# Projecting keys and queries head by head, with high and low parts stacked on 128 partitions

## The chip, the cores and the metric

The kernel runs on one core of one Trainium2 chip. Its engines are TensorE (PE in the profile; PEld is its loading of weights, which overlaps the matmuls), VectorE (DVE), ScalarE (ACT), GpSimd (POOL) and SyncE (SP), which issues the DMAs here. The metric is device time in microseconds for one execution; lower is better.

## The reference

Linear attention for 8 batches of 8 heads, 576 positions, head dimension 64, 128 features, and then a feed-forward block with a gated depthwise convolution, all in float32:

```python
def phi(x):
    proj = np.einsum('bhsd,df->bhsf', x, w_phi)                  # 64 -> 128
    proj = proj - np.max(np.abs(proj), axis=-1, keepdims=True)
    return np.concatenate([np.exp(proj), np.exp(-proj)], axis=-1)
q_p, k_p = phi(q), phi(k)
kv = np.einsum('bhsf,bhsd->bhfd', k_p, v)
z = np.sum(k_p, axis=2)
num = np.einsum('bhsf,bhfd->bhsd', q_p, kv)
den = np.einsum('bhsf,bhf->bhs', q_p, z)[..., None] + 1e-06
x = num / den                                                    # heads joined: 576 x 512
h = np.maximum(x @ w_in, 0.0)                                    # 512 -> 1024
# conv_out: three taps of conv_w along the positions
out = (h / (1.0 + np.exp(-conv_out))) @ w_out                    # 1024 -> 512
```

The change concerns the first line of `phi`, for q and for k.

## The kernel before, in words

The host lays q and k out transposed, two heads above each other on the 128 partitions (64 dimensions each), and passes the projection weights as `wbd`, a 128 x 256 block-diagonal matrix: `w_phi` in the upper left for the first head, `w_phi` in the lower right for the second.

Most products are made in float32r, a data type that TensorE multiplies in one pass with fewer bits. To keep the accuracy each operand is split into a high part (rounded to float32r) and a low part (what is left), and three products are added up in PSUM: high by high, high by low, low by high. Some products use plain float32 instead; the profile then shows two records for each matmul. The profile prints `f32` for both types when it comes to TensorE.

The work of a batch is cut into two units `qd`, and each unit into five chunks `g`: chunk 0 has one block of 128 columns, chunks 1 to 4 have two blocks each, so a unit has nine blocks for k and nine for q. A block holds 128 positions of two heads. For each chunk:

- `load_split` (L180, L183) loads the chunk on SP's queue, and POOL makes the high part (L62, `kxh`, `qxh`) and the low part (L65, `kxl`, `qxl`). For q in the first two units (`NQ_F32`) there is no split.
- `project` multiplies. The data are the stationary operand (the weights of the PE array), `wbd` is the moving one. A block takes three matmuls of 256 columns (L203, L204, L205), or one in plain float32 (L200). DVE then takes the greatest absolute value (L208) and subtracts it (L210).
- For k, ACT takes the two exponentials, and TensorE multiplies with v into `kv` (L255, L259, plain float32).
- For q, TensorE transposes (L324), ACT takes the exponentials, high and low parts are made, and TensorE forms numerator and denominator `nm` (L352 plain float32, L360 float32r). The `kv` matmuls of the unit after are put between these by hand, by an order chain (`after`).

The denominators go by DMA into one small tile (L381), DVE takes reciprocals, and a DMA brings them back (L402); TensorE spreads them over the partitions (L410). Then the feed-forward block follows for half a batch at a time: 96 matmuls `hp` (L435), ReLU on ACT (L442) into a ring of `NH` tiles, the convolution on POOL and DVE (L458, L463), the sigmoid, the gating, and 96 matmuls `op` (L494). Its weights arrive as 64-bit words; POOL, DVE and ACT convert and split them during the first part of the run (`weight_process`, tile `w_t`).

The order in which all this is issued comes from a planner in the kernel file: generators for each chunk announce how long TensorE will be busy (`yield pe(330 * n)` for a projection of n blocks) and what they wait for, and the planner takes attention and feed-forward steps in proportion to what is left of each (`ATT_PE`, `MOE_PE`). The framework's scheduler then orders each engine's queue by these priorities.

Of the kernel before, what the change touches and what calls it, by code (L numbers as in the profile page):

```python
# [16 lines left out]
F = 128  # L17
# [6 lines left out]
NH = 11  # L24
# [11 lines left out]
def kernel(  # L36
# [44 lines left out]
    selr_f = sb.tile([P, P], F32, name="selr_f", tag="qr", bufs=2)  # L81
# [75 lines left out]
    def pe(ns):  # L157
        return ("pe", ns)
# [17 lines left out]
    def load_split(src, b, qd, g, kind):  # L176
        c0, n = group_columns(g)
        if kind == "q" and 2 * b + qd < NQ_F32:
            raw = sb.tile([P, n * P], F32, name=f"{kind}r{b}_{qd}_{g}", tag=kind + "xh", bufs=2)
            nc.sync.dma_start(out=raw, in_=src[b, qd, :, c0 : c0 + n * P])  # L180
            return n, raw, None
        raw = sb.tile([P, n * P], F32, name=f"{kind}r{b}_{qd}_{g}", tag=kind + "r", bufs=2)
        nc.sync.dma_start(out=raw, in_=src[b, qd, :, c0 : c0 + n * P])  # L183
# [5 lines left out]
    def project(n, hi, lo, b, qd, g, kind):  # L189

        if b == 0 and kind == "k":

            ps = pm.tile([P, n * 256], F32, name=f"{kind}p{b}_{qd}_{g}", tag="m")
        else:
            ps = pg.tile([P, n * 256], F32, name=f"{kind}p{b}_{qd}_{g}", tag="g", bufs=4)
        for t in range(n):
            o = ps[:, t * 256 : (t + 1) * 256]
            his = hi[:, t * P : (t + 1) * P]
            if lo is None:
                nc.tensor.matmul(out=o, lhsT=his, rhs=wbd_f, start=True, stop=True)  # L200
                continue
            los = lo[:, t * P : (t + 1) * P]
# [10 lines left out]
    def after(ins, trace):  # L213
# [3 lines left out]
        with tc.issue_after(ins.ins):  # L217
            return trace()
# [430 lines left out]
```

## Time and profile before

| | |
|---|---|
| time, median of 3 runs | 837.99 us (837.19 to 838.23) |
| the profiled execution, span from its first to its last instruction | 955.3 us (no other time of that execution is given) |
| mean granted TensorE clock in the profile | 0.750 of full speed |
| busy: PE, PEld, DVE, ACT, POOL | 937.9, 920.7, 622.2, 576.6, 294.1 us |
| instructions | 18005, of them 6414 matmuls and 6414 weight loads |

The profiled execution is longer than the timed runs; the profile says at which clock it ran, and nothing says so for the timed runs. Matmuls are pipelined: the duration of a matmul's record overlaps its neighbours', so the mean duration of a group isn't what a matmul costs. The cost is read from runs of matmuls one after another, from the chain of work that ended last, or from a window's share. In rows of groups the columns are line, engine, operation, tiles, shapes (for TensorE: weight rows x weight columns, then rows x moving columns), count, busy us, mean ns, idle time before and who ended it.

### The profile page before, as it was taken

The numbers are of one execution on the slowest core, as the hardware profiler recorded it, in microseconds if no ns is written. First come the engines' busy times: TensorE is split into PE (matmuls) and PEld (weight loads), VectorE is DVE, ScalarE is ACT, GpSimd is POOL, SyncE is SP. The second block draws the span as 40 slices with busy tenths as digits, with TensorE's granted clock in tenths as the row PEclk, the third lists the DMA queues.
The fourth block names the chain that finished last, engine by engine and source line by source line (L and its number), as shares of the span: only waits on it lengthen the run. The fifth ranks groups of instructions, "written<-read, shape, count | busy, mean of one in ns | idle before, by whom it ended". The sixth has DMA issues, their size and how long they took to land.

```text
span 955.3 us, 18005 instructions
## 1 busy us (share of the span) xinstructions
PE 937.9 (98%) x6414; PEld 920.7 (96%) x6414; DVE 622.2 (65%) x1326; ACT 576.6 (60%) x1228; POOL 294.1 (31%) x469
## 2 busy tenths in 40 slices
PE   8999899999999999999999999999999999999998
PEld 7887799999999999999999999999999999999998
DVE  6789986887767557576665656756667575555441
ACT  4787876866667555765647556675666647533322
POOL 5668753433323213131322312313123220111010
PEclk8677777777777777777777777777777777777777
DMA  5543321112112111111211101121111100000001
GB/s 169 173 136 117 96 57 47 41 37 58 40 49 58 33 50 38 44 54 31 57 32 52 53 25 56 37 62 38 39 52 28 38 5 21 15 19 26 20 20 37
DMA packets 56336, 49.19 MB, mean 51 GB/s; under 512 B 15028, under 2 KB 54200, under 8 KB 56248
## 3 DMA queue, kind: packets, MB, share of 16 engines
q1 hardware_dynamic: 56248, 48.05, 17.5%
q8 instruction: 51, 0.84, 0.4%
q14 instruction: 37, 0.30, 0.1%
HBM read 38.14 MB, written 9.44 MB: 50 GB/s over the span
## 4 chain that ended last, share of the span: by engine, by line
PE 93%; DVE 3%; ACT 2%; issue 1%; DMA 1%; POOL 0%; SPq 0%; ACTq 0%
PE op L494 26%; PE hp L435 25%; PE kv L259 10%; PE nm L360 9%; PE tp L324 4%; PE nm L352 3%; PE kp L203 2%; PE kp L204 2%; PE kp L205 2%; PE qp L204 2%; PE qp L203 2%; PE qp L205 2%; PE kv L255 2%; PE rb L410 1%; PE qp L200 1%
## 5 line engine op out<-in xcount | busy, mean ns | idle before, releaser
L259 PEld LDWEIGHTS kv<-v,ke 128*128 128x128 f32 x1024 | 181.8, 221 | 5.2
L259 PE MATMUL kv<-v,ke 128*128 128x65 f32 x1024 | 181.8, 280 | 0.0
L463 DVE SCALAR_TENSOR_TENSOR c<-h,cw,c 128x287 f32<-128x287 f32 (+1 forms) x256 | 138.6, 550 | 59.1 <-POOL c L458 57.3
L435 PE MATMUL hp<-xl,win_hi 128*128 128x290 f32 x512 | 171.0, 334 | 0.0
L435 PE MATMUL hp<-xh,win_hi 128*128 128x290 f32 x512 | 170.9, 335 | 0.1
L494 PE MATMUL op<-gh,wout_hi 128*128 128x288 f32 x512 | 170.5, 333 | 0.0
L494 PE MATMUL op<-gh,wout_lo 128*128 128x288 f32 x512 | 170.3, 333 | 0.0
L494 PE MATMUL op<-gl,wout_hi 128*128 128x288 f32 x512 | 170.3, 333 | 0.0
L435 PE MATMUL hp<-xh,win_lo 128*128 128x290 f32 x512 | 170.1, 332 | 0.0
L458 POOL TENSOR_SCALAR c<-h,cw 128x288 f32<-128x288 f32 x128 | 73.0, 571 | 264.1 <-ACT h L442 234.6
L62 POOL TENSOR_SCALAR kxh<-kr 128x256 fp32r<-128x256 f32 (+1 forms) x80 | 38.6, 482 | 259.0 <-PE kp L204 252.6
L65 DVE TENSOR_TENSOR ql<-qe,qh 128x512 fp32r<-128x512 f32 x112 | 77.6, 707 | 45.7 <-ACT qh L60 45.6
L435 PEld LDWEIGHTS hp<-xh,win_hi 128*128 128x128 f32 x512 | 104.4, 205 | 1.0 <-ACT os L499 0.6
L435 PEld LDWEIGHTS hp<-xh,win_lo 128*128 128x128 f32 x512 | 104.2, 204 | 0.2
L435 PEld LDWEIGHTS hp<-xl,win_hi 128*128 128x128 f32 x512 | 103.6, 202 | 0.2
L494 PEld LDWEIGHTS op<-gh,wout_hi 128*128 128x128 f32 x512 | 103.7, 203 | 0.0
L494 PEld LDWEIGHTS op<-gh,wout_lo 128*128 128x128 f32 x512 | 103.5, 202 | 0.1
L442 ACT ACTIVATE h<-hp 128x290 f32<-128x290 f32 x128 | 52.4, 411 | 84.4 <-PE hp L435 83.9
L494 PEld LDWEIGHTS op<-gl,wout_hi 128*128 128x128 f32 x512 | 103.2, 202 | 0.1
L378 ACT ACTIVATE dr<-nm 1x512 f32<-1x512 f32 (+1 forms) x96 | 46.3, 483 | 77.7 <-PE nm L360 48.6
L208 DVE TENSOR_REDUCE km<-kp 128x4 f32<-128x512 f32 (+1 forms) x80 | 50.6, 633 | 59.5 <-PE kp L205 59.1
L330 ACT ACTIVATE qe<-tp 128x512 f32<-128x512 f32 x112 | 61.7, 597 | 39.0 <-PE tp L324 37.3
(88 smaller groups left out, 2125.1 us busy)
## 6 DMA issues: line engine op xcount, KB each, us to landing
v<-in_vt_dram SPq DMA_DIRECT2D x80, 130.0 KB
out_dram<-os SPq DMA_DIRECT2D x64, 144.0 KB
qr<-in_qT_dram SPq DMA_DIRECT2D x64, 128.0 KB
kr<-in_kT_dram SPq DMA_DIRECT2D x64, 128.0 KB
w_r<-in_w_in_dram SPq DMA_DIRECT2D x8, 512.0 KB
w_r<-in_w_out_dram SPq DMA_DIRECT2D x8, 512.0 KB
rr<-rc SPq DMA_DIRECT2D x128, 2.2 KB
qr<-in_qT_dram SPq DMA_DIRECT2D x16, 64.0 KB
```

What stands on the lines that cost most here:

```text
L62: nc.gpsimd.tensor_scalar(out=hi, in0=src, scalar1=1.0, scalar2=0.0, op0=ALU.mult, op1=ALU.add)
L65: eng_lo.tensor_tensor(out=lo, in0=src, in1=hi.bitcast(F32), op=ALU.subtract)
L208: nc.vector.tensor_reduce(out=m, in_=ps3, axis=AX, op=ALU.max, apply_absolute_value=True)
L259: ins = nc.tensor.matmul(out=kp[i][:, s, p0 : p0 + VW], lhsT=lhsT, rhs=v[:, (2 * t + i) * VW : (2 * t + i + 1) * VW], start=False, stop=(g ...
L330: nc.scalar.activation(out=e, in_=tp.rearrange("p i t s -> p i (t s)"), func=AF.Exp, scale=1.0 - 2.0 * s)
L360: ins = after(ins, lambda: nc.tensor.matmul(out=ps[:, i, o : o + w], lhsT=w_, rhs=x_, start=(k == 0), stop=(k == 5)))
L378: nc.scalar.activation(out=dro.rearrange("o (r i c) -> o i r c", i=2, c=16), in_=ps[D : D + 1, :, o : o + w].rearrange("o i (r c) -> o i r ...
L435: nc.tensor.matmul(out=ps, lhsT=w_, rhs=x_, start=(k == 0), stop=(k == 11))
L442: nc.scalar.activation(out=hs, in_=ps, func=AF.Relu)
L458: nc.gpsimd.tensor_scalar(out=cv, in0=hs[:, o : o + TC], scalar1=cw[:, f, 1:2], scalar2=0.0, op0=ALU.mult, op1=ALU.add)
L463: nc.vector.scalar_tensor_tensor(out=cv[:, lo:hi], in0=hs[:, o + j - 1 + lo : o + j - 1 + hi], scalar=cw[:, f, j : j + 1], in1=cv[:, lo:hi ...
L494: nc.tensor.matmul(out=ps, lhsT=w_, rhs=x_, start=(k == 0), stop=(k == 23))
```

## The change

Each head is projected by itself. A block's data are laid out so that one head's high part stands on partitions 0 to 63 and its low part on partitions 64 to 127, 128 columns. Stacked so, one pass against `w_phi`'s high part written twice above itself gives high by high plus low by high, and a second pass against the low part written twice gives high by low plus low by low. A block of two heads takes four matmuls of 128 moving columns, where three of 256 stood.

For that, each chunk is loaded twice, once to the upper and once to the lower 64 partitions, with the two heads side by side in the columns (two DMAs, each of the full size). POOL makes the high part over all 128 partitions and twice the columns, and then the low part over the lower 64 partitions and twice the columns. The weights come by three DMAs into one tile, `wst_f`, and are split into `wst`, high part left, low part right. In the plain float32 chunks the same doubled layout is multiplied with `w_phi` above zeros. The raw tiles of k and q share one ring of three (`r`), where each kind had two. The ring of `h` tiles goes from 11 to 10. The planner's figure for a projection goes from 330 to 225 a block. `after` is only moved in the file.

```diff
-NH = 11
+NH = 10
...
-    wbd_f = cp.tile([P, 2 * F], F32, name="wbd_f")
+    wst_f = cp.tile([P, 2 * F], F32, name="wst_f")
     with tc.high_priority():
-        nc.sync.dma_start(out=wbd_f, in_=wbd)
-    wbd_hi = cp.tile([P, 2 * F], F32R, name="wbd_hi")
-    wbd_lo = cp.tile([P, 2 * F], F32R, name="wbd_lo")
-    split(wbd_f, wbd_hi, wbd_lo, nc.vector, nc.vector)
+        nc.sync.dma_start(out=wst_f[:D, :F], in_=wbd[:D, :F])
+        nc.sync.dma_start(out=wst_f[D:, :F], in_=wbd[D:, F:])
+        nc.sync.dma_start(out=wst_f[:, F:], in_=wbd[:, :F])
+    wst = cp.tile([P, 2 * F], F32R, name="wst")
+    split(wst_f[:, :F], wst[:, :F], wst[:, F:], nc.vector, nc.vector)
...
     def load_split(src, b, qd, g, kind):
         c0, n = group_columns(g)
+        w = 2 * n * P
+
+        def load(raw):
+            for h in range(2):
+                nc.sync.dma_start(out=raw[D * h : D * h + D].rearrange("d (i c) -> d i c", i=2),
+                                  in_=src[b, qd, :, c0 : c0 + n * P].rearrange("(i d) c -> d i c", i=2))
+
         if kind == "q" and 2 * b + qd < NQ_F32:
-            raw = sb.tile([P, n * P], F32, name=f"{kind}r{b}_{qd}_{g}", tag=kind + "xh", bufs=2)
-            nc.sync.dma_start(out=raw, in_=src[b, qd, :, c0 : c0 + n * P])
-            return n, raw, None
-        raw = sb.tile([P, n * P], F32, name=f"{kind}r{b}_{qd}_{g}", tag=kind + "r", bufs=2)
-        nc.sync.dma_start(out=raw, in_=src[b, qd, :, c0 : c0 + n * P])
-        hi = sb.tile([P, n * P], F32R, name=f"{kind}xh{b}_{qd}_{g}", tag=kind + "xh", bufs=2)
-        lo = sb.tile([P, n * P], F32R, name=f"{kind}xl{b}_{qd}_{g}", tag=kind + "xl", bufs=2)
-        split(raw, hi, lo, nc.gpsimd, nc.gpsimd)
-        return n, hi, lo
+            raw = sb.tile([P, w], F32, name=f"{kind}r{b}_{qd}_{g}", tag=kind + "x", bufs=2)
+            load(raw)
+            return n, raw
+        raw = sb.tile([P, w], F32, name=f"{kind}r{b}_{qd}_{g}", tag="r", bufs=3)
+        load(raw)
+        x = sb.tile([P, w], F32R, name=f"{kind}x{b}_{qd}_{g}", tag=kind + "x", bufs=2)
+        nc.gpsimd.tensor_scalar(out=x, in0=raw, scalar1=1.0, scalar2=0.0, op0=ALU.mult, op1=ALU.add)
+        nc.gpsimd.tensor_tensor(out=x[D:], in0=raw[D:], in1=x[D:].bitcast(F32), op=ALU.subtract)
+        return n, x
...
-        for t in range(n):
-            o = ps[:, t * 256 : (t + 1) * 256]
-            his = hi[:, t * P : (t + 1) * P]
-            if lo is None:
-                nc.tensor.matmul(out=o, lhsT=his, rhs=wbd_f, start=True, stop=True)
-                continue
-            los = lo[:, t * P : (t + 1) * P]
-            nc.tensor.matmul(out=o, lhsT=his, rhs=wbd_hi, start=True, stop=False)
-            nc.tensor.matmul(out=o, lhsT=his, rhs=wbd_lo, start=False, stop=False)
-            nc.tensor.matmul(out=o, lhsT=los, rhs=wbd_hi, start=False, stop=True)
+        for j in range(2 * n):
+            t, i = divmod(j, 2)
+            o, xs = ps[:, j * F : (j + 1) * F], x[:, (i * n + t) * P : (i * n + t + 1) * P]
+            if x.dtype == F32:
+                nc.tensor.matmul(out=o, lhsT=xs, rhs=wst_f[:, F:], start=True, stop=True)
+            else:
+                nc.tensor.matmul(out=o, lhsT=xs, rhs=wst[:, :F], start=True, stop=False)
+                nc.tensor.matmul(out=o, lhsT=xs, rhs=wst[:, F:], start=False, stop=True)
...
-        yield pe(330 * n)
+        yield pe(225 * n)
...
-    ATT_PE = B * (18 * 330 + 72 * 215 + 18 * 550 + 8 * 6 * 270 + 4 * 250)
+    ATT_PE = B * (18 * 225 + 72 * 215 + 18 * 550 + 8 * 6 * 270 + 4 * 250)
```

More of the change, by code (lines that the diff above doesn't have):

```diff
@@ L71, in load_const @@
         return t
-    wbd_f = cp.tile([P, 2 * F], F32, name="wbd_f")
+    wst_f = cp.tile([P, 2 * F], F32, name="wst_f")
     with tc.high_priority():
-        nc.sync.dma_start(out=wbd_f, in_=wbd)
-    wbd_hi = cp.tile([P, 2 * F], F32R, name="wbd_hi")
-    wbd_lo = cp.tile([P, 2 * F], F32R, name="wbd_lo")
-    split(wbd_f, wbd_hi, wbd_lo, nc.vector, nc.vector)
+        nc.sync.dma_start(out=wst_f[:D, :F], in_=wbd[:D, :F])
[3 more added lines that the diff above has]
+    split(wst_f[:, :F], wst[:, :F], wst[:, F:], nc.vector, nc.vector)
     idn = load_const(ident, [P, P], "idn")
-    selr_f = sb.tile([P, P], F32, name="selr_f", tag="qr", bufs=2)
+    selr_f = sb.tile([P, P], F32, name="selr_f", tag="r", bufs=3)
     nc.gpsimd.memset(selr_f, 0.0)
@@ L177, in load_split, with after, project @@
         c0, n = group_columns(g)
-        if kind == "q" and 2 * b + qd < NQ_F32:
-            raw = sb.tile([P, n * P], F32, name=f"{kind}r{b}_{qd}_{g}", tag=kind + "xh", bufs=2)
-            nc.sync.dma_start(out=raw, in_=src[b, qd, :, c0 : c0 + n * P])
-            return n, raw, None
-        raw = sb.tile([P, n * P], F32, name=f"{kind}r{b}_{qd}_{g}", tag=kind + "r", bufs=2)
-        nc.sync.dma_start(out=raw, in_=src[b, qd, :, c0 : c0 + n * P])
-        hi = sb.tile([P, n * P], F32R, name=f"{kind}xh{b}_{qd}_{g}", tag=kind + "xh", bufs=2)
-        lo = sb.tile([P, n * P], F32R, name=f"{kind}xl{b}_{qd}_{g}", tag=kind + "xl", bufs=2)
-        split(raw, hi, lo, nc.gpsimd, nc.gpsimd)
-        return n, hi, lo
-    def project(n, hi, lo, b, qd, g, kind):
+        w = 2 * n * P
[3 more added lines that the diff above has]
+                                  in_=src[b, qd, :, c0 : c0 + n * P].rearrange("(i d) c -> d i c", i=2))
+        if kind == "q" and 2 * b + qd < NQ_F32:
+            raw = sb.tile([P, w], F32, name=f"{kind}r{b}_{qd}_{g}", tag=kind + "x", bufs=2)
[7 more added lines that the diff above has]
+        return n, x
+    def after(ins, trace):
+        if ins is None:
+            return trace()
+        with tc.issue_after(ins.ins):
+            return trace()
+    def project(n, x, b, qd, g, kind):
         if b == 0 and kind == "k":
@@ L211, in project @@
         return pr
-    def after(ins, trace):
-        if ins is None:
-            return trace()
-        with tc.issue_after(ins.ins):
-            return trace()
     kv = {}
@@ L230, in k_process @@
         yield until(back("kp", 2), back("kv", 4))
-        n, hi, lo = load_split(kT, b, qd, g, "k")
+        n, x = load_split(kT, b, qd, g, "k")
         v0 = 16 if g == 0 else 4 * (g - 1)
@@ L237, in k_process @@
         set_ready(("kp", j))
-        pr = project(n, hi, lo, b, qd, g, "k")
+        pr = project(n, x, b, qd, g, "k")
         e = sb.tile([P, 2, 2 * n, F], F32, name=f"ke{b}_{qd}_{g}", tag="ke", bufs=2)
@@ L310, in q_process @@
         yield until(back("qp", 2))
-        n, hi, lo = load_split(qT, b, qd, g, "q")
+        n, x = load_split(qT, b, qd, g, "q")
         yield wait(3000)
@@ L314, in q_process @@
         set_ready(("qp", *divmod(j, 5)))
-        pr = project(n, hi, lo, b, qd, g, "q")
-        yield pe(330 * n)
+        pr = project(n, x, b, qd, g, "q")
+        yield pe(225 * n)
         yield wait(1700)
```

## The prediction

> **What bounds the kernel now.** I read the page first: span, the busy share of each engine, the chain that ended last.
>
> ```profile
> span 955.3 us, 18005 instructions
> PE 937.9 (98%) x6414; PEld 920.7 (96%) x6414; DVE 622.2 (65%) x1326; ACT 576.6 (60%) x1228; POOL 294.1 (31%) x469
> PE 93%; DVE 3%; ACT 2%; issue 1%; DMA 1%; POOL 0%; SPq 0%; ACTq 0%
> ```
>
> TensorE is nearly always busy and carries 93% of the chain. The weight loads (PEld) are busy almost as long as the matmuls, and there is one load for each matmul: 6414 and 6414. So I ask which of the two ends last where the projections run. Next the busy times by stretch (columns: window, its length, PE, PEld, DVE, ACT, POOL busy with counts, granted clock, DMA share, GB/s), then the chain of 200 to 830 us and the counts of projection matmuls in it.
>
> ```profile
> 48.00:100.00 52.00, 49.43 (x295) 42.35 (x294) 45.24 (x82) 41.64 (x88) 39.01 (x41) 0.74 0.43 124
> ...
> 200.00:830.00 630.00, 630.00 (x4451) 628.04 (x4450) 407.32 (x894) 391.65 (x838) 163.90 (x293) 0.75 0.15 41
> ```
>
> ```profile
> by line: PE op L494 27.0%; PE hp L435 26.9%; PE nm L360 12.1%; PE kv L259 11.1%; PE tp L324 4.5%; PE qp L204 2.4%; PE qp L203 2.3%; PE kp L204 2.2%; PE qp L205 2.2%; PE kp L203 2.1%; PE nm L352 2.0%; PE kp L205 2.0%; PE kv L255 1.9%; PE rb
> L203 PE MATMUL qp<-wbd_hi,qxh 128*128 128x256 f32 x99 | 31.3, 326 | 0.0
> L203 PE MATMUL kp<-wbd_hi,kxh 128*128 128x256 f32 x92 | 31.1, 339 | 0.0
> ```
>
> From 200 to 830 us TensorE has no gap at all at a granted clock of 0.75, while DVE, ACT and POOL are busy for 407, 392 and 164 of 630 us. There a nanosecond of TensorE is a nanosecond of the kernel. The six projection lines take 2.4+2.3+2.2+2.2+2.1+2.0 = 13.2% of that stretch, 83.2 us, for 191 blocks (99+92) of three matmuls: 435 ns a block, 145 ns a matmul. The mean durations of the matmul rows (326 and 339 ns) overlap and are not this cost.
>
> **What a matmul costs on this chip.** The windows' columns here are PE busy, PEld busy, clock; the next two rows are from the chain (start, length, what), the last three the weight loads (shortest/median/longest ns).
>
> ```profile
> 19.94:21.96 2.02, 2.02 (x14) 1.98 (x14) 0.75 0.07 12
> 28.07:31.27 3.20, 3.20 (x16) 3.20 (x16) 0.50 0.47 166
> ```
>
> ```profile
> 140.35 0.58 PE nm L352 x8
> ```
>
> ```profile
> 441.85 9.44 PE op L494 x59
> ```
>
> ```profile
> L259 PEld LDWEIGHTS kv<-v,ke x1024: 186/225/338, 13.4 to 773.3; 128*128 128x128 f32 x171
> L360 PEld LDWEIGHTS nm<-qh,kvh x224: 134/139/227, 101.8 to 819.5; 128*65 128x65 f32 x112
> L203 PEld LDWEIGHTS kp<-wbd_hi,kxh x144: 186/198/338, 5.1 to 762.1; 128*128 128x128 f32 x144
> ```
>
> Streaming: the op run is 9.44 us for 59 matmuls of 288 columns, 160 ns each, 0.556 ns a column; so 256 columns stream in 142 ns and 128 in 71 ns. Loading: the first two rows are back-to-back kv matmuls (L259), 65 moving columns against 128 weight columns: 2.02/14 = 144 ns each at clock 0.75 and 3.20/16 = 200 ns at 0.50. The nm run (L352) has the same data type and 64 moving columns, but 65 weight columns: 0.58/8 = 72 ns. Nearly the same stream, half the weights, half the time: the kv run goes at the pace of its weight loads, 144 ns for 128 weight columns. Does a float32r load cost the same as the plain float32 of kv? The projections' load (L203) is 186 ns at the shortest, kv's 186, and the 65-column float32r load (L360) 134. The two 128-column kinds agree, so I take 144 ns for both. A matmul's slot is then the longer of its own stream and of the load of the next one's weights. The present projection sits at balance: stream 142, next load 144, measured 145.
>
> The Trainium skill, "TensorE: Matmul & The Clock Gate", section "LDWEIGHTS (loading the stationary operand)", gives a load as columns / 1.2 ns, 107 ns for 128 columns; divided by the clock of 0.75 this is an estimate of 142 ns, and the kv row agrees.
>
> **The change, part by part.**
>
> *Projection matmuls.* A block (128 columns of two heads) goes from three matmuls of 256 columns to four of 128: 768 streamed columns to 512, but three weight loads to four. The two matmuls on the same x slice don't share a load: L203 and L204 share hi now, and the loads number as many as the matmuls. A new slot is 144 ns where the next weights are 128 wide, 72 ns where they are the 65 of nm. How often that is, the chain shows:
>
> ```profile
> 405.02 0.15 PE kp L203
> 405.18 0.15 PE kp L204
> 405.33 0.17 PE kv L259 x2
> 405.50 0.18 PE kp L205
> 405.68 0.12 PE nm L360
> 405.80 0.15 PE kp L203
> 405.95 0.17 PE kv L259 x2
> 406.12 0.22 PE qp L203
> 406.33 0.16 PE qp L204
> 406.49 0.12 PE qp L205
> 406.61 0.16 PE qp L203
> 406.77 0.15 PE kp L204
> 406.92 0.12 PE nm L360
> ```
>
> Of nine projection matmuls two are followed by nm. With that mix a block costs 4 x (7/9 x 144 + 2/9 x 72) = 512 ns against 435: +77 ns. There are 144 + 126 = 270 float32r blocks (16 units of nine, less two units of q in plain float32): +20.8 us. Upper end: every successor is 128 wide, 576 ns, +141, +38 us. Lower end: every second successor short, 432 ns, -3 ns, -1 us. I take the 77, the rate of the row.
>
> *The plain float32 q blocks* (two units, L200):
>
> ```profile
> L200 PE MATMUL qp<-wbd_f,qr 128*128 128x256 f32 x36 | 12.8, 496 | 4.6 <-DMA qr<-in_qT_dram 4.1 <-ACT qh L330 0.5
> ```
>
> 36 records for 18 blocks: two a matmul, at nm's 72 ns per 64 columns 288 ns each, 576 a block. After: two heads x two records of 128 columns, 144 ns of stream, 144 of load: 576. Nothing.
>
> *Splits on POOL and loads.* hi is made over twice the columns, lo over twice the columns on half the partitions.
>
> ```profile
> L62 POOL TENSOR_SCALAR kxh<-kr 128x256 fp32r<-128x256 f32 x64 | 32.6, 509 | 221.6 <-PE kp L204 218.6 <-DMA kr<-in_kT_dram 2.1 <-PE kv L255 0.8
> L62 POOL TENSOR_SCALAR kxh<-kr 128x128 fp32r<-128x128 f32 x16 | 6.0, 376 | 37.4 <-PE kp L204 34.0 <-DMA kr<-in_kT_dram 3.2
> L65 POOL TENSOR_TENSOR kxl<-kr,kxh 128x256 fp32r<-128x256 f32 x64 | 51.0, 797 | 3.4 <-PE kp L205 1.0
> L109 POOL TENSOR_TENSOR w_t<-w_t 128x512 f32<-128x512 f32 x16 | 22.7, 1417 | 11.1 <-DVE w_t L107 7.4 <-DMA rr<-rc 3.0 <-DVE rc L64 0.6
> 48.00:100.00 52.00, 9.59 (x14) 0.74 0.43 124
> 48.00:100.00 52.00, 5.27 (x16) 3.04 (x16) 6.60 (x11) 0.74 0.43 124
> ```
>
> Hi at 512 columns: 509 + 2 x (509 - 376) = 775 ns; lo: the 512-column subtraction row, 1417. A chunk goes from 1306 to 2192 ns, +0.9 us; the 120 large chunks make 106 us, the 30 small ones less than a fifth of that. From 200 us on POOL has 466 idle us and its splits wait for TensorE (218.6 us): hidden. From 48 to 100 us it is not so clear: POOL is busy 39.0 of 52, and the last two rows (what touches kr; what touches qr) show 14 + 11 split instructions, 12.5 chunks, +11.3 us: 50.3 of 52, beside the weight conversion on the same queue. I take +3 us, ends 0 (the 13 idle us take it) and +8 (most of the 11.3 shows, since DVE, at 45 of 52, waits on POOL's results too).
>
> ```profile
> L183 SPq DMA_DIRECT2D kr<-in_kT_dram x80: 327/339/1165, 2.1 to 719.8; - x80
> ACT h L442 <- PE hp L435: 83.9, 68, 2.7
> ```
>
> Each chunk's load becomes two DMAs of full size: 160 more issues at 0.34 us, 54 us on SP's queue, at a DMA share of 0.15 in the long stretch: hidden. The raw tiles go from two per kind to three for both; SP waits for POOL to free one, and with POOL slower it will wait longer, with the stores and the den and rr transfers queued behind. DVE waits for den, TensorE after it; the zero gaps of TensorE cover that, and I cost it at nothing, +5 us if that cover goes. At the start, two more small weight loads and one more issue ahead of the first q and k chunk: 3 x 0.34, +1 us. NH 11 to 10: the h copies on ACT wait for TensorE alone (second row), not for a buffer; nothing, and at worst a short wait of ACT under TensorE's other work. The planner's 225 for 330 only reorders TensorE's queue, which is full in either order. The split of the weights halves two DVE instructions at the start: nothing.
>
> **Sum.** In the profiled execution +20.8 + 3 + 1 = 24.8 us on a span of 955.3; no own time stands beside the span. The median of the runs is 837.99, 0.877 of it; no row shows their clock. Since TensorE's time goes with the clock, I scale its term: 20.8 x 0.877 = 18.2, and leave the other 4: 838 + 22 = 860 us. Its own range: PE -1 to +33, the rest 0 to +10, 837 to 881.
>
> **The rivals.**
>
> *Columns decide, faster.* If the narrow float32r matmuls' loads hide better than kv's, a block costs 4 x 71 = 284 ns, -151, -40.8 us, scaled -35.8: with the 4 us above, 806. For it: the total stream falls and no row shows a float32r load binding by itself. Against: the 186 ns floor shared by both kinds. It decides once a load falls below 435/4 = 109 ns.
>
> By the Trainium skill, same page, section "Back-to-back issue gap", a warm matmul takes N/2.4 + 2.5 ns, 55.8 for 128 columns and 109.2 for 256; as an estimate 4 x 55.8 against 3 x 109.2, so this rival. The kv row, 144 ns for 65 columns, does not follow that formula.
>
> *Interleaving covers the loads, about no change.* The scheduler mixes projections with nm and kv; at every second successor short a block is level (432 ns), and only POOL and the start remain: 838 to 846.
>
> *Narrow float32r runs like plain float32, much slower.* Every float32r matmul in this trace streams at least 256 columns. If 128 columns run as the L200 rows do, in two records, a block has eight slots of 144: 1152, +717, +194 us, scaled +170: about 1012. For it speaks only that no row excludes it.
>
> **How the numbers follow.** Forecast 0.60; columns decide 0.16; covered 0.15 (0.04 faster, 0.05 same, 0.06 slower); like float32 0.09. About 0.2% (1.7 us) is what a measurement of this kernel tells from no change. Faster 0.16 + 0.04 = 0.20, same 0.05, slower 0.60 + 0.06 + 0.09 = 0.75. The range reaches down to 822, where about half of the first rival's chance lies above it, and up to 884: left out are 0.09 and about 0.08.
>
> **What would show it.** Projection loads x1080 with a 186 ns floor, and projection lines that take more of the chain in the long stretch (above 15%) with 125 to 145 ns a matmul: the load bound. Near 75 ns a matmul: the first rival. Two records a matmul: the last. POOL near 50 of 52 us between 48 and 100 with TensorE's gaps grown there: the POOL term. I am wrong if float32r loads of this shape run faster than kv's, or if the order pairs them with nm far more often.

## The result, and the profile after

The changed kernel takes 890.80 us (median of 4 runs, 887.75 to 893.78) against 837.59 us (4 runs, 836.79 to 838.23) on the same chip: a ratio of 1.0637 (95% interval 1.0612 to 1.0663), 53 us slower. The forecast was 860 us, with a range of 822 to 884: the sign is right, the time lies above the range.

The profile of before that the prediction read ran at a clock of 0.75. To compare at one clock, the unchanged kernel was profiled again (`e0_before`, below: 838.14 us, span 836.4, clock 0.986). The changed kernel's profiled run took 890.75 us, span 888.9, clock 0.964. First the page of the changed kernel, then that of the unchanged one: span, busy times, the chain that ended last.

```profile
span 888.9 us, 18763 instructions
PE 836.7 (94%) x6720; PEld 823.3 (93%) x6720; DVE 676.8 (76%) x1326; ACT 570.8 (64%) x1228; POOL 421.9 (47%) x469
PE 61%; DVE 18%; ACT 8%; DMA 6%; issue 4%; POOL 2%; SPq 1%; POOLq 0%; ACTq 0%; DVEq 0%
```

```profile
span 836.4 us, 18005 instructions
PE 799.5 (96%) x6414; PEld 781.4 (93%) x6414; DVE 623.8 (75%) x1326; ACT 573.0 (69%) x1228; POOL 308.1 (37%) x469
PE 77%; DVE 8%; ACT 7%; DMA 4%; issue 3%; POOL 1%; SPq 0%; POOLq 0%; DVEq 0%; ACTq 0%
```

TensorE is busy for 37.2 us more and idle for 15.3 us more (52.2 against 36.9). In the traces of these two runs the granted clock is always either 0.5 or 1.0, so the means of 0.964 and 0.986 are 64 and 23 us at half clock; of the 37.2 us up to 20 are that (an estimate, as if TensorE had work in all of it). The timed runs agree: 0.960 to 0.967 in the changed kernel, 0.979 to 0.990 in the unchanged one. The 306 further matmuls are the 270 of the float32r blocks and 36 records of the plain float32 q blocks. DVE runs the same 1326 instructions, yet is busy for 53 us more, and its share of the chain goes from 8% to 18%. That was in no step of the prediction. The stretches (window in us, its length, PE, PEld, DVE, ACT, POOL busy, clock, DMA share, GB/s) show where; the changed kernel first, then the unchanged one.

```profile
0.00:30.00 30.00, 18.60 (x121) 18.35 (x122) 9.09 (x18) 7.40 (x15) 14.66 (x24) 0.94 0.52 146
30.00:120.00 90.00, 72.64 (x506) 66.05 (x506) 75.66 (x128) 64.82 (x139) 65.84 (x59) 0.86 0.53 159
120.00:200.00 80.00, 74.20 (x585) 72.44 (x585) 75.32 (x132) 56.72 (x121) 59.27 (x56) 0.88 0.33 93
200.00:300.00 100.00, 95.79 (x797) 94.61 (x796) 82.85 (x165) 72.10 (x157) 48.78 (x56) 0.97 0.26 72
300.00:700.00 400.00, 392.61 (x3307) 391.00 (x3306) 315.03 (x629) 272.27 (x586) 196.29 (x221) 0.99 0.25 72
```

```profile
0.00:30.00 30.00, 21.56 (x136) 19.36 (x137) 19.86 (x39) 14.13 (x28) 16.59 (x33) 0.94 0.61 181
30.00:120.00 90.00, 73.97 (x504) 63.66 (x503) 78.34 (x137) 72.76 (x153) 65.78 (x65) 0.91 0.42 123
120.00:200.00 80.00, 75.58 (x632) 73.99 (x630) 70.92 (x148) 62.63 (x137) 37.72 (x57) 0.98 0.19 51
200.00:300.00 100.00, 98.45 (x839) 97.86 (x838) 79.00 (x170) 73.13 (x160) 37.79 (x61) 1.00 0.20 57
300.00:700.00 400.00, 397.61 (x3316) 395.36 (x3315) 300.29 (x660) 286.27 (x615) 133.48 (x223) 1.00 0.17 48
```

Up to 300 us TensorE has made 2009 matmuls in the changed kernel and 2111 in the unchanged one, although the changed one needs more of them for the same work. In this early part DVE was close to full already (70.9 of 80 us between 120 and 200 us) and is now at 75.3, and the granted clock falls (0.86 and 0.88 against 0.91 and 0.98). Two neighbouring pieces of the changed kernel show what that does:

```profile
125.70:139.30 13.60, 10.50 (x93) 9.83 (x92) 13.60 (x20) 11.42 (x23) 13.18 (x10) 1.00 0.37 101
139.30:153.00 13.70, 11.99 (x62) 11.54 (x60) 13.51 (x22) 7.03 (x16) 11.56 (x11) 0.50 0.41 124
```

DVE is busy throughout, TensorE has gaps in the first piece, and in the second, at half clock, it makes 62 matmuls where it made 93. Here a lost wait seems to be paid twice, once as a gap and once as slower matmuls behind it; no run isolates this. The Trainium skill, "TensorE: Matmul & The Clock Gate", section "HAM oscillation — how this bites in real kernels", ties a halved clock to gaps of TensorE longer than about 3.4 us. The halving agrees, the length of the gap does not: between 126 and 153 us no wait of TensorE was over 2.0 us.

The matmul count is also a ledger (a running account of who is behind) for those experiments that keep the number of matmuls: the unchanged kernel makes 3316 in 400 us, 0.121 us each, and what another kernel is behind at 300 us and again at 700 us, times 0.121, is its loss by stage.

### The profile page after: what moved, and what is told of

Read it like the earlier page. It is cut to its first block, busy times and chain, and to the rows that moved or that the text cites. A ratio compares the mean times of both kernels' runs of the same rounds, so it can differ in the third digit from the quotient of the medians.

```text
span 888.9 us, 18763 instructions
## 1 busy us (share of the span) xinstructions
PE 836.7 (94%) x6720; PEld 823.3 (93%) x6720; DVE 676.8 (76%) x1326; ACT 570.8 (64%) x1228; POOL 421.9 (47%) x469
## 4 chain that ended last, share of the span: by engine, by line
PE 61%; DVE 18%; ACT 8%; DMA 6%; issue 4%; POOL 2%; SPq 1%; POOLq 0%; ACTq 0%; DVEq 0%
PE op L504 19%; PE hp L445 18%; PE nm L370 6%; PE kv L269 6%; PE tp L334 3%; DMA den<-dr 2%; PE kp L221 2%; PE kp L222 2%; PE qp L222 2%; PE qp L221 2%; DVE qm L225 2%; DVE ql L65 2%; DVE km L225 2%; DVE c L473 1%; DVE ks L227 1%
## 5 line engine op out<-in xcount | busy, mean ns | idle before, releaser
L269 PEld LDWEIGHTS kv<-v,ke 128*128 128x128 f32 x1024 | 158.6, 198 | 3.1 <-issue 0.2
L504 PE MATMUL op<-gh,wout_hi 128*128 128x288 f32 x512 | 153.9, 301 | 1.0 <-ACT os L509 0.9
L445 PE MATMUL hp<-xl,win_hi 128*128 128x290 f32 x512 | 154.4, 302 | 0.0
L504 PE MATMUL op<-gl,wout_hi 128*128 128x288 f32 x512 | 152.4, 298 | 0.0
L504 PE MATMUL op<-gh,wout_lo 128*128 128x288 f32 x512 | 152.2, 297 | 0.0
L197 POOL TENSOR_SCALAR kx<-kr 128x512 fp32r<-128x512 f32 (+1 forms) x80 | 54.6, 685 | 127.0 <-PE kp L222 67.4
L198 POOL TENSOR_TENSOR kx<-kr,kx 64x512 fp32r<-64x512 f32 (+1 forms) x80 | 100.4, 1257 | 5.1
L250 ACT ACTIVATE ke<-ks 128x512 f32<-128x512 f32 (+1 forms) x80 | 46.9, 586 | 86.9 <-DVE ks L227 86.3
L221 PE MATMUL kp<-wst,kx 128*128 128x128 f32 x288 | 77.9, 291 | 15.9 <-POOL kx L198 11.4
L198 POOL TENSOR_TENSOR qx<-qr,qx 64x512 fp32r<-64x512 f32 (+1 forms) x70 | 90.1, 1287 | 4.3
```

The costliest lines, as they stand in the source:

```text
L197: nc.gpsimd.tensor_scalar(out=x, in0=raw, scalar1=1.0, scalar2=0.0, op0=ALU.mult, op1=ALU.add)
L198: nc.gpsimd.tensor_tensor(out=x[D:], in0=raw[D:], in1=x[D:].bitcast(F32), op=ALU.subtract)
L221: nc.tensor.matmul(out=o, lhsT=xs, rhs=wst[:, :F], start=True, stop=False)
L250: nc.scalar.activation(out=e[:, 0], in_=pr, func=AF.Exp)
L269: ins = nc.tensor.matmul(out=kp[i][:, s, p0 : p0 + VW], lhsT=lhsT, rhs=v[:, (2 * t + i) * VW : (2 * t + i + 1) * VW], start=False, stop=(g ...
L445: nc.tensor.matmul(out=ps, lhsT=w_, rhs=x_, start=(k == 0), stop=(k == 11))
```

## The experiments

Each ratio is to the kernel before on the same chip. Where a cost is given in us below, it is the ratio less one, times the 838 us of before. The code below is shortened to the lines that matter.

Each change also makes the scheduler order the queues anew, so a change of order is part of every cost below. With the shared ring alone (`y2_ring3`) only 2811 of TensorE's 5660 matmuls (plain float32 ones counted once) write a tile of the same name at the same place as before, and that costs 0.03%. The four runs that change next to no work (`y1_nh10`, `y2_ring3`, `x4_before_225`, `z3_before_150`) lie between -0.58% and +0.34%; in the changed kernel the planner's figure alone is worth 1.7%.

| run | what it has of the change | median us | ratio (95% interval) |
|---|---|---|---|
| p1_four_narrow | four matmuls of 128 columns | 864.57 | 1.0317 (1.0291 to 1.0344) |
| p1b_four_wide | four matmuls, but of 256 columns | 868.37 | 1.0375 (1.0360 to 1.0391) |
| x1_wide_pool | the wider splits on POOL | 859.63 | 1.0273 (1.0256 to 1.0291) |
| y4_wide_late | these from the fifth of 16 units on | 855.49 | 1.0204 (1.0182 to 1.0226) |
| z4_wide_later | these from the ninth unit on | 842.15 | 1.0054 (1.0037 to 1.0070) |
| x2_double_dma | doubled rearranged loads, ring of three, NH 10 | 864.79 | 1.0340 (1.0306 to 1.0373) |
| z1_plain_double | the same with plain loads | 848.50 | 1.0128 (1.0109 to 1.0146) |
| w2_double_one_load | the same bytes in one plain load | 842.54 | 1.0074 (1.0045 to 1.0103) |
| y3_two_halves | two plain loads of half the bytes each | 842.11 | 1.0043 (1.0014 to 1.0072) |
| z2_long_issues | two rearranged loads of half the bytes each | 844.45 | 1.0081 (1.0060 to 1.0102) |
| y1_nh10 | NH 10 | 840.94 | 1.0034 (1.0021 to 1.0047) |
| y2_ring3 | ring of three | 837.85 | 1.0003 (0.9982 to 1.0024) |
| x4_before_225 | the planner's 225 | 832.31 | 0.9942 (0.9922 to 0.9962) |
| z3_before_150 | a planner's 150 | 834.99 | 0.9974 (0.9959 to 0.9989) |
| p2_wide_loads | changed kernel, old matmuls, planner's 330 | 892.45 | 1.0646 (1.0616 to 1.0675) |
| p3_after_330 | changed kernel, planner's 330 | 904.87 | 1.0808 (1.0766 to 1.0849) |
| w1_after_one_load | changed kernel, one plain load a chunk | 884.24 | 1.0552 (1.0531 to 1.0573) |

### The unchanged kernel again

Nothing is changed.

> The kernel before, unchanged, profiled once more. Its first profile ran at a granted clock of 0.75 and was 955 us long, while the runs take 838; the changed kernel's profile ran at 0.964 and is as long as its runs. If the profile of before simply fell in a throttled stretch, this one shows about 836 us at a clock near 0.96, with TensorE's weight-bound slots at 107 ns instead of 144 and TensorE no longer free of gaps between 200 and 800 us (I expect 5 to 10% idle). If 838 us at full clock also has no gaps, the chain is TensorE alone and every added slot counts in full.

It took 838.14 us, beside a median of 837.65 for the kernel before on the same chip. Its profile, at a clock of 0.986, is the one to which all others are compared.

### The matmuls alone: narrow, and wide

```diff
-  matmul(out=o, lhsT=his, rhs=wbd_hi) ; matmul(out=o, lhsT=his, rhs=wbd_lo) ; matmul(out=o, lhsT=los, rhs=wbd_hi)
+  for i in range(2):                                  # p1_four_narrow: 128 columns each
+      matmul(out=oi, lhsT=his, rhs=wi) ; matmul(out=oi, lhsT=los, rhs=wi)      # wi = wbd_hi[:, i * F : (i + 1) * F]
+  for wi in (wbd_hi, wbd_lo):                         # p1b_four_wide: 256 columns each
+      matmul(out=o, lhsT=his, rhs=wi) ; matmul(out=o, lhsT=los, rhs=wi)
```

> The kernel before with its loads and splits, but each block takes four matmuls of 128 columns (high and low part of the data against the high part of the weights, head by head) in place of three of 256; the product of high data and low weights is left out. Only TensorE's work changes. Weight-bound slots: one more slot of about 107 ns in each of 270 blocks, +15 to +29 us, 853 to 867. If the slower time came from POOL, loads and start alone: 838 within 3 us. If columns decided: about 820.

> The kernel before with four matmuls of 256 columns a block (high and low data against high and low weights) in place of three: against the run with four of 128 columns the weight loads are equal and the streamed columns double. If a slot is the longer of stream (107 ns for 256 columns at full clock) and load (107 ns): 865 within 5 us, as with 128 columns. If streamed columns added to the load: +29 us or more over that, 893 and up.

Loads, splits and planner are those of before. The narrow form costs 26.6 us, the wide one 31.4: in all, halving the columns gives back only 5 us. The chains of both around 400 us (start, length, what); the narrow kernel first.

```profile
400.32 0.11 PE tp L325
400.43 0.06 PE kp L205
400.49 0.11 PE qp L205
...
401.53 0.12 PE kp L205
401.65 0.11 PE kp L206
401.75 0.11 PE kp L205
401.86 0.11 PE kp L206
```

```profile
405.19 0.12 PE qp L204
405.32 0.12 PE qp L205
405.44 0.12 PE qp L204
405.55 0.12 PE qp L205
```

One after another, matmuls of 128 columns take 0.11 us and those of 256 take 0.12: in such a row nearly the same, as a weight load that sets the pace would have it. Where narrow ones stand between others the step in the chain can be 0.06.

Rows of their own kind are the exception, so the mean has to come from a count. Between 300 and 700 us all three kernels run at a clock of 1.00. First the stretch in the narrow and in the wide kernel (the unchanged one stands above), then the projections' weight loads in it, k and q of the unchanged, of the narrow and of the wide kernel.

```profile
300.00:700.00 400.00, 399.42 (x3392) 396.90 (x3392) 298.84 (x642) 276.95 (x602) 135.46 (x222) 1.00 0.18 50
300.00:700.00 400.00, 395.28 (x3282) 391.81 (x3281) 293.72 (x624) 270.99 (x589) 131.17 (x216) 1.00 0.17 48
```

```profile
300.00:700.00 400.00, 35.14 (x213) 1.00 0.17 48
300.00:700.00 400.00, 35.65 (x228) 1.00 0.17 48
```

```profile
300.00:700.00 400.00, 45.79 (x288) 1.00 0.18 50
300.00:700.00 400.00, 44.43 (x288) 1.00 0.18 50
```

```profile
300.00:700.00 400.00, 45.32 (x280) 1.00 0.17 48
300.00:700.00 400.00, 45.08 (x284) 1.00 0.17 48
```

The unchanged kernel makes 441 projection matmuls (147 blocks of three) and 2875 others, the narrow one 576 (144 blocks of four) and 2816, the wide one 564 (141 blocks) and 2718. So the narrow kernel falls behind by 59 others and 3 blocks, 68 matmuls of the unchanged kernel or 8.2 us: 57 ns for each of its blocks. The wide one falls behind by 157 others and 6 blocks, 175 matmuls or 21.1 us: 150 ns a block. (4.7 us of the wide kernel's loss are waits; in the other two TensorE waits for 0.6 and 2.4 us.) In this stretch halved columns are therefore worth 13 us. The narrow kernel loses part of that before 300 us: its clock between 30 and 120 us is 0.81, against 0.90 in the wide kernel and 0.91 in the unchanged one, and its timed runs have a mean clock of 0.968 to 0.976, those of the wide one 0.986 to 0.988.

57 ns over 270 blocks is 15.4 us. The other 11 of the 26.6 us don't come out of this rate. Part of them is the lower clock:

```profile
30.00:120.00 90.00, 75.14 (x480) 66.74 (x481) 77.80 (x128) 66.98 (x142) 61.12 (x64) 0.81 0.39 119
```

75.1 us busy at 0.81 are 61 at full clock, against 67 us in the unchanged kernel (74.0 at 0.91): some 6 us, an estimate. Why the clock was lower there wasn't tried.

### The wider splits alone

```diff
-  split(raw, hi, lo, nc.gpsimd, nc.gpsimd)
+  twice = raw.unsqueeze(1).broadcast_to([P, 2, n * P])          # x1; y4: only where 2 * b + qd >= 4; z4: >= 8
+  nc.gpsimd.tensor_scalar(out=x, in0=twice, scalar1=1.0, scalar2=0.0, op0=ALU.mult, op1=ALU.add)
+  nc.gpsimd.tensor_tensor(out=x[D:], in0=twice[D:], in1=x[D:].bitcast(F32), op=ALU.subtract)
```

> The kernel before with POOL's splits as wide as in the changed kernel (high part over twice the columns, low part over twice the columns on half the partitions), but each chunk still loaded once by one DMA, raw tiles, NH and the three matmuls of 256 columns as before; x is read so that the projections are not those of the reference. POOL theory (POOL's extra 110 us slow DVE's instructions and hold the weight conversion back): +25 to +45 us, 863 to 883, DVE's busy time near 690 us. Load theory (twice the DMAs, longer issues and the shared ring): 838 to 846.

> The wide-POOL run (860), with the wide splits only from the fifth unit on, that is after the weights are converted (about 124 us); the first four units of k and q are split as before. Theory that POOL's extra work costs only in the first part, where it holds the weight conversion and the first chunks back: 838 to 845. Theory that it costs all along, by DVE's slower instructions: 855 to 860, since 12 of 16 units stay wide.

> The wide-POOL run with wide splits only from the ninth unit on (about 290 us). In the run with wide splits from the fifth unit the loss of 17 us stood at 12 when the second half batch reached op and at 16 by 350 us, and grew no more. If POOL's work costs only while DVE is the busiest engine besides TensorE, up to about 300 us: 838 to 842. If it costs all along: half of 22, 849.

Matmuls and loads are those of before; POOL's two instructions for each chunk get wider. The two parts also share one tile now, so that a chunk's first matmul may have to wait for both. That hardly matters: the first matmul of a chunk of k comes 12 us (median) after its low part is ready, in the unchanged kernel as in this one. Wide splits everywhere cost 22.9 us, from the fifth unit on 17.1 us, from the ninth on 4.5 us. The first and last starts of the wide k splits in the two partial kernels (fifth unit, then ninth; shortest/median/longest ns, first to last start):

```profile
L189 POOL TENSOR_SCALAR kx<-kr x60: 405/622/1314, 112.3 to 672.9; 128x512 fp32r<-128x512 f32 x48, 128x256 fp32r<-128x256 f32 x12
```

```profile
L189 POOL TENSOR_SCALAR kx<-kr x40: 404/619/1312, 280.2 to 662.5; 128x512 fp32r<-128x512 f32 x32, 128x256 fp32r<-128x256 f32 x8
```

So, if the costs add, about 12.6 us (17.1 less 4.5) belong to the chunks split between about 112 and 280 us, 5.8 to those before, 4.5 to all those after; the three kernels ran on three chips. The way from POOL to TensorE goes over DVE. DVE's groups (after the bar: busy us, mean ns of one, then idle time before and who ended it), unchanged kernel first, then the kernel with wide splits:

```profile
L65 DVE TENSOR_TENSOR ql<-qe,qh 128x512 fp32r<-128x512 f32 x112 | 82.1, 747 | 36.4 <-ACT qh L60 36.4
L463 DVE SCALAR_TENSOR_TENSOR c<-h,cw,c 128x288 f32<-128x288 f32 x128 | 69.1, 543 | 18.4 <-POOL c L458 17.5
L208 DVE TENSOR_REDUCE km<-kp 128x4 f32<-128x512 f32 x64 | 43.6, 681 | 20.1 <-PE kp L205 20.1
L210 DVE TENSOR_TENSOR ks<-kp,km 128x512 f32<-128x512 f32 x64 | 43.5, 680 | 0.5
```

```profile
L65 DVE TENSOR_TENSOR ql<-qe,qh 128x512 fp32r<-128x512 f32 x112 | 92.9, 844 | 13.9 <-ACT qh L60 13.8
L464 DVE SCALAR_TENSOR_TENSOR c<-h,cw,c 128x288 f32<-128x288 f32 x128 | 90.3, 709 | 13.6 <-POOL c L459 12.4
L209 DVE TENSOR_REDUCE km<-kp 128x4 f32<-128x512 f32 x64 | 43.7, 683 | 23.4 <-PE kp L206 23.2
L211 DVE TENSOR_TENSOR ks<-kp,km 128x512 f32<-128x512 f32 x64 | 43.5, 680 | 0.4
```

The same DVE instructions last longer where all their data lie in SBUF (747 to 844 ns, 543 to 709), and not where they read a projection out of PSUM (681 to 683, 680 to 680). In all DVE is busy for 691.5 us against 623.8. The traces show that it is POOL that lengthens them: those of the first row that no POOL instruction overlaps take 682 ns in the unchanged kernel (63 of 112) and 676 in the other (38), those that one overlaps take 831 and 930. The reduction out of PSUM (third row) takes 676 to 683 either way. The Trainium skill, "SBUF — State Buffer", section "SBUF: two separate sides", says that a DVE instruction with two SBUF inputs and a GpSimd instruction that reads SBUF lock each other out for a whole instruction. These rows agree with it. TensorE's two largest waits in this kernel name DVE (us in total, times, longest); the largest in the unchanged kernel that names DVE stands below:

```profile
PE hp L436 <- DVE xl L65: 5.1, 2, 3.4
PE tp L325 <- DVE qs L211: 4.6, 6, 1.9
```

```profile
PE kp L203 <- DVE ks L210: 3.3, 3, 1.5
```

All waits of TensorE that name DVE come to 28.6 us, against 9.2 in the unchanged kernel, where the span is shorter by 20.4 us.

Whether a longer DVE instruction costs depends on how full DVE is. The kernel that starts at the fifth unit, between 200 and 300 us, and below it the unchanged one:

```profile
200.00:250.00 50.00, 45.75 (x363) 44.09 (x362) 43.19 (x80) 32.81 (x70) 21.34 (x24) 0.97 0.17 48
250.00:300.00 50.00, 47.65 (x400) 46.86 (x400) 46.06 (x86) 37.05 (x80) 27.42 (x31) 1.00 0.21 59
```

```profile
200.00:250.00 50.00, 49.55 (x425) 49.42 (x424) 40.99 (x88) 36.45 (x80) 19.98 (x32) 1.00 0.20 57
250.00:300.00 50.00, 48.90 (x416) 48.45 (x416) 38.01 (x83) 36.68 (x81) 17.81 (x29) 1.00 0.20 56
```

DVE comes to 43 and 46 of 50 us, and TensorE makes 363 and 400 matmuls where 425 and 416 stood. Of the 6.6 us that TensorE waits there, 4.8 name DVE. POOL itself is half idle (27 of 50). Later, between 300 and 700 us, the wide kernel's DVE is at 336.6 of 400 us and its TensorE still makes 3289 matmuls (3316 before): there the lengthening is nearly hidden. By the ledger the wide kernel is 137 matmuls behind at 300 us (1974 against 2111), 16.5 us, and loses another 27, 3.3 us, up to 700; the sum, 19.8, is nearly the whole difference of the spans (856.8 - 836.4 = 20.4).

### The loads alone, and what it is in them

```diff
 # x2_double_dma: the change's ring, NH = 10 and loads; splits and three wide matmuls on half of the columns
 # z1_plain_double: the same, but
+  nc.sync.dma_start(out=raw[:, h * n * P : (h + 1) * n * P], in_=src[b, qd, :, c0 : c0 + n * P])     # h = 0, 1
 # w2_double_one_load: the same, but (the host lays the chunk out as raw)
+  nc.sync.dma_start(out=raw, in_=src[b, qd, :, 2 * c0 : 2 * c0 + w])
 # y3_two_halves: the kernel before, but
+  nc.sync.dma_start(out=raw[D * h : D * h + D], in_=src[b, qd, D * h : D * h + D, c0 : c0 + n * P])  # h = 0, 1
 # z2_long_issues: the kernel before, but
+  nc.sync.dma_start(out=raw[D * h : D * h + D].rearrange("d (i c) -> d i c", i=2),
+                    in_=src[b, qd, :, c0 + h * m : c0 + h * m + m].rearrange("(i d) c -> d i c", i=2))  # m = n * P // 2
```

> The kernel before with the changed kernel's loads (two DMAs of full size for each chunk, raw tiles of twice the columns in one ring of three, NH 10), but POOL's splits and the matmuls as before on half of what was loaded; the projections are not those of the reference. Load theory: +25 to +45 us, 863 to 883, and op of the first half batch late as in the wide-loads run. POOL theory: 838 to 850, DVE's busy time near 624 us.

> The doubled-loads run (865) with its two DMAs a chunk as plain ones: each fills one half of the columns on all 128 partitions from the same rows, so bytes, number of issues, ring of three and NH 10 stay, and only the split into 64 partitions with two pieces a row goes, whose issue takes SP 0.61 us instead of 0.34. The first half of each raw tile is what POOL splits; the projections are those of the reference but for the missing low part of the weights. If the long issues cost: 845 to 850. If the bytes cost: 862 to 867.

> The kernel before with doubled bytes for each chunk, but in one plain transfer laid out by the host (ring of three raw tiles, 10 h tiles, wide PE matmuls as before). Its projections read only one head of each pair and leave the low part of the weights out, so that its output is not the reference's; the numbers and shapes of instructions on the other engines are those of the kernel before. If issues and the shape of the transfers are the cost of the loads, only the 2.8 us of the smaller h ring stay: 838 to 842 us. If the bytes are the cost: 848 us, as with two plain loads, up to 865 us, as with two rearranged loads.

> The kernel before with each split chunk loaded by two DMAs of 64 partitions, so that the bytes stay the same and SP issues 150 more. Theory that the number of issues on SP's queue costs: 845 or more. Theory of the shared ring or of the bytes: 838 within 3 us.

> The kernel before with each split chunk loaded by two DMAs of the long kind (64 partitions, two pieces a row), each with half of the columns, so that the bytes stay as before; rings, NH and splits as before; the columns come in another arrangement, so the output is not that of the reference. If the long issues on SP's queue cost: 850 to 860. If the bytes cost: 842, as with two plain half loads.

And the two small parts, `NH = 10` alone (`y1_nh10`) and the shared ring `tag="r", bufs=3` alone (`y2_ring3`):

> The kernel before with the ring of h tiles at 10 instead of 11, nothing else. It is part of what the doubled loads run changed. If the ring matters: 843 or more. If ACT never waits for an h tile: 838 within 2 us.

> The kernel before with k's and q's raw tiles in one ring of three instead of two rings of two; the tiles keep their size and each chunk one DMA. Theory that the shared ring costs (SP waits at the head of its queue for POOL, and the weight loads and the transfers of den and rr stand behind it): 845 to 860. Theory that bytes and issues of the doubled loads cost: 838 within 4 us.

The smaller h ring costs 0.34%, the shared ring nothing that can be told. Doubled bytes in one plain transfer, with both of these in it, cost 0.74%: the bytes as such are worth about 0.4%. Two plain transfers 1.28%, two rearranged ones 3.40%. An issue on SP is longer in the rearranged form; k's loads of the kernels with the two rearranged double loads, with one plain double load, and with the two plain halves:

```profile
L182 SPq DMA_DIRECT2D kr<-in_kT_dram x160: 595/602/1244, 2.0 to 668.5; - x160
```

```profile
L181 SPq DMA_DIRECT2D kr<-in_kT_dram x80: 327/332/1531, 1.6 to 647.6; - x80
```

```profile
L184 SPq DMA_DIRECT2D kr<-in_kT_dram x160: 465/547/1698, 2.4 to 642.3; - x160
```

0.60 us in the median, not the 0.34 that the prediction took from the plain load. The time that SP spends on it is not the whole cost, though: the two rearranged halves (`z2_long_issues`, median 610 ns) have as many issues of that length and cost 0.81%, against 0.43% for two plain halves (their intervals overlap). In these two kernels the queues of TensorE, DVE and POOL hold the same instructions in the same order. Between `x2_double_dma` and `w2_double_one_load` the orders differ (on TensorE 3368 of 5660 matmuls write a tile of the same name at the same place). So for the 2.7% between these two, the longer issues and the new order aren't separated. In which stretches the time goes is plain: `x2_double_dma` is 140 matmuls behind at 300 us, 16.9 us (49 of them in the first 30 us, 110 between 120 and 200), and loses 79 more, 9.5 us, up to 700; 26.4 of the 26.5 us by which its span is longer.

### The planner's figure

```diff
-        yield pe(330 * n)
+        yield pe(225 * n)      # x4_before_225; 150 * n in z3_before_150; and in ATT_PE likewise. p3_after_330: the changed kernel with 330
```

> The kernel before with only the planner's figure changed, 225 for 330. In the changed kernel the same figure was worth 14 us. If it is a better order for attention as such: 825 to 834. If it only mends a queue that the loads and splits hold back: 838 within 3 us.

> The kernel before with the planner's figure for a projection at 150 instead of 330 (225 gave 832). If a lower figure keeps giving attention more room: 826 to 831. If 225 was a lucky order: 832 to 840.

> The changed kernel with the planner's old figure for a projection (330 a block instead of 225, also in its total for attention). If the planner's figure, which promises TensorE time that it doesn't get, carries part of the 53 us, this comes 5 to 20 us under 891. If it only reorders, 891 within 4 us.

With 225 the kernel before gets 0.58% faster: 832.31 us, the fastest of all these kernels. The changed kernel would be 14 us slower without it (904.87 against 890.80), where I had expected it to be as fast or 5 to 20 us faster. 150 gives about half as much (0.26%). Three matmuls of 0.12 us in a row are 360 ns a block, more than any of these figures, so a truer figure isn't what helps; the order is another one, and by how much an order is better wasn't predictable from the profile.

### The parts together

```diff
 # p2_wide_loads: the changed kernel, but for each block
+            matmul(out=o, lhsT=his, rhs=wbd_hi) ; matmul(out=o, lhsT=his, rhs=wbd_hi) ; matmul(out=o, lhsT=los, rhs=wbd_hi)
 # w1_after_one_load: the changed kernel, but for each chunk (the host lays it out as raw)
+            nc.sync.dma_start(out=raw, in_=src[b, qd, :, 2 * c0 : 2 * c0 + w])
```

> The kernel before with the changed kernel's loads and splits (twice the DMAs, twice the columns on POOL, three raw tiles shared by k and q, NH 10), but three matmuls of 256 columns against the high part of the weights as before; the projections are therefore not those of the reference. TensorE's work is that of before. If TensorE's slots explain the result: 838 to 845. If POOL, loads and the start carry it: +20 to +35 us, 858 to 873, with DVE busy near 670 us instead of 622 and the first projection of k near 22 us instead of 9.

> The changed kernel with one load for each chunk in place of two: the host lays each chunk out as it is to stand on the 128 partitions (both heads side by side, and a copy of that below), so that one plain transfer of the same number of bytes as the two brings it. SP issues 160 loads in place of 320, and none rearranged. If the issues (their number and their 0.6 us each) and the shape of the transfers are what the loads cost, then about 25 us of the 28 us that the doubled loads cost alone go, and what stays is the matmuls, the wider splits and the planner's figure: 865 us (860 to 872). If the doubled bytes cost it, little goes: 880 to 890 us. If both count as in the doubled plain loads (10.7 us with one issue twice as often), then about 873 us.

Loads and splits together, with three wide matmuls, cost 6.46%, 54 us where I had expected 20 to 35; alone they cost 3.40% and 2.73%, 6.13% in sum. These two add up, and with the matmuls of before they are as slow as the whole change. TensorE's wait of 32.6 us more (idle 69.5 us, 890.6 - 821.1, against 36.9) is most of it. The four narrow matmuls on top (`p3_after_330`) add 12.4 us, not 26.6: they may have gone into gaps that TensorE had anyway, but no run shows it.

With one plain load in the changed kernel I expected 865 us; it took 884.24. So the rearranged loads, worth 2.7% against one plain load when alone, are worth only 0.85% in the changed kernel (1.0637 against 1.0552, from two chips). The time lies where I had put it for a cost of the bytes, yet alone the bytes cost about 0.4%. The stretches tell more; here the long one of this kernel:

```profile
300.00:700.00 400.00, 399.90 (x3409) 398.43 (x3408) 328.08 (x641) 279.67 (x605) 202.69 (x225) 1.00 0.27 75
```

From 300 to 700 us it makes 102 matmuls more than the changed kernel (3409 against 3307), some 12 us. By 300 us it is 57 behind (1952 against 2009), some 7 us, and its clock is 0.83 from 30 to 120 us and 0.84 from 120 to 200, against 0.86 and 0.88. So the plain load does gain in the long stretch, and the early part takes half of it back; why the clock is lower there wasn't tried. What stays there agrees with the sum of the others: 3.17% (matmuls), 2.73% (splits), 0.74% (one double load) less 0.58% to 1.6% for the planner is 5.0 to 6.1%, and 5.52% was measured.

## Why the prediction was right or wrong

**The matmuls: right in direction and rate, too small in all.** In rows of their own kind the slot model held: narrow matmuls take 0.11 us and wide ones 0.12. At the mean the step from the old block to the new one was taken as 77 ns at a clock of 0.75, 58 ns at full clock; the count gives 57. But by the same working four wide matmuls should cost 64 ns a block more than four narrow ones (576 against 512), 48 at full clock, and in the long stretch they cost 93 more (150 against 57). That the two kernels came out within 5 us of each other, as was expected of them, is partly luck, by the lower clock of the narrow one. The term of 18.2 us measured 26.6, since some 11 us came on top of the rate, part of it as a lower clock. The loads came out as foretold, 1080 of them with a shortest of 186 ns. The rival "columns decide" is out: the narrow form is slower. The Trainium skill, "TensorE: Matmul & The Clock Gate", section "Back-to-back issue gap", gives the formula used for this rival for a single matmul alone and says beside it that it counts too little at small widths, with no budget for weight loads; the 0.11 us of a row, against its 0.056, agree with that. "Narrow float32r runs like plain float32" is out too: the matmuls number 6720, one record for each float32r matmul. So is "interleaving covers the loads": matmuls alone cost 3.17%.

**The splits: the failed step.** The prediction priced the instructions well: 775 and 1417 ns for the wide forms, and 777 and 1449 in `x1_wide_pool` (728 and 1375 in the changed kernel). What failed is "From 200 us on POOL has 466 idle us and its splits wait for TensorE (218.6 us): hidden", and the +3 us for 48 to 100 us. Idle time of POOL was the wrong cover to count. POOL's instructions lengthen DVE's, and DVE was nearly full up to about 300 us. Between 48 and 100 us, where the prediction feared a POOL at 50 of 52 us, it is at 35.1; it comes nearest to full after that (45.1 of 50 between 100 and 150). The term measured 22.9 us instead of 3, more than half of it between about 112 and 280 us. The step holds only for the long stretch after that: 4.5 us for half of all chunks.

**The loads: the other failed step.** "54 us on SP's queue, at a DMA share of 0.15 in the long stretch: hidden", with 0.34 us an issue, and +1 us for the start. The issue took 0.60, and the loads with ring and h ring cost 28.5 us when alone. A share of transfer time doesn't tell how long an issue holds SP's queue. "At the start ... +1" was 49 matmuls, 6 us, in `x2_double_dma`, and 15 matmuls in the changed kernel (121 against 136 in 30 us). How much of the rest is the issue's length and how much the new order stays open; in the changed kernel, one plain load gives back 0.85%.

**The clock: read at one value, and left out.** The cover was read in a profile at 0.75, where DVE is busy for 65% of the long stretch (407 of 630 us). At a clock of 1.00 DVE is busy for 79 of 100 us between 200 and 300 and for 75% after that: TensorE got faster and DVE didn't (busy for 622.2 and 623.8 us in all), so there was less cover than the prediction saw. And a wait of TensorE was priced as a gap alone. The rows up to 300 us add up to 54 us at half clock in the changed kernel and 23 in the unchanged one; that is up to 15 us (an estimate) inside the costs of the parts, for which the prediction has no term.

**NH and the planner.** Both were costed at nothing; they are 2.8 us and -4.9 us in the kernel before (the planner's figure -14 us in the changed one). The ring at nothing was right. The plain float32 q blocks at nothing weren't tried alone.

**The sum.** 18.2 + 3 + 1 was forecast; alone the parts measured 26.6, 22.9 and 28.5, less 4.9, 73 us together, of which 53 show. In the order of the runs it is 54 us for loads and splits, 12 for the narrow matmuls on top, less 14 for the planner's figure. The upper end of the range held only 0 to +10 us for all that isn't TensorE (its own terms end at 8, 1 and 5, which is 14), and that bound is what the result passed: loads and splits were over five times as much.

## What to carry to other kernels

Count weight loads as well as columns: here a third less of streamed columns with one load more for each block made TensorE slower, by 57 ns a block. Read cover in each stage, at the clock of the timed runs, and on each engine that shares something with the one made busier: here an idle POOL hid nothing, because its instructions held up a DVE that was nearly full. Ask what a wait does to the clock behind it. Parts tried alone name the causes, but a scheduler sorts all queues anew for each edit, and the parts' costs needn't add up.

## What the runs showed of the hardware that was not expected

- DVE instructions with all their data in SBUF lengthened from 543 to 709 ns and from 747 to 844 when POOL's splits were wider; those that read PSUM stayed at 680. Of the 112 `ql` instructions there, those without a POOL instruction beside them took 676 ns, those with one 930.
- The issue of a load rearranged over two dimensions took SP 0.60 us (median), that of a plain one over 128 partitions 0.33 (0.42 where each chunk has two of them), over 64 partitions 0.55.
- A narrow projection can take a step of 0.06 us between other matmuls, and 0.11 in a row of its own kind.
- In the changed kernel the granted clock was 0.5 from 139.3 to 153.0 us, with no wait of TensorE over 2.0 us between 126 and 153.
- A matmul of 288 columns in a row (`op`) took 160 ns at a clock of 0.75 and 133 at 1.00 (6.53 us for 49): it did not follow the clock in full.
